# Attention and two MLPs in one kernel: places of their own, by tables, for attention's jobs and a step's operations

## The chip, the cores and the metric

The kernel runs on one core of a Trainium2 chip. The metric is the device time of one execution in microseconds. Three runs of the kernel before took 1445.11, 1445.52 and 1445.93 us; the median is 1445.52.

## The reference

Attention of 8 batches, 8 heads, 576 positions, head size 64, through 32 packed tokens per head, and then two MLPs on the 4608 tokens (width 512, hidden 2048), all in fp32:

```python
a = softmax(p @ k.T / 8) @ v          # 32 packed tokens per head
x = softmax(q @ a.T / 8) @ a          # 576 positions per head
h = x @ moe_w_in
g = where(h >= 1, h, where(h <= -1, 0, (h + 1)**2 / 4))
x = g @ moe_w_out
h = x @ moe2_w_in
out = (h * sigmoid(h)) @ moe2_w_out
```

## The kernel before

**Two stages.** The first stage (to about 750 us) computes attention and the first MLP, the second the second MLP (products of L842 and L904 on blocks of 512 and 384 tokens). The change touches the first stage alone. There the first MLP's input product is folded: the attention output is a weighted sum of 32 packed tokens per head, so the packed tokens are multiplied with `w_in` first (`wp8`, L566, and `wp_out`, L581, for each quarter f of the hidden width), and a step then multiplies the attention weights with the result.

**Steps.** One step is one half t of a batch (288 tokens) and one slice m of 128 hidden units: 8 x 2 x 16 = 256 steps, 32 per batch. Its operations are `a_h` (6 matmuls, L661, on TensorE), `a_relu` (two activations on ScalarE, L676 and L677), `a_max` (VectorE, L682), `a_hi` (ScalarE, L686) and `a_lo` (VectorE, L692), which split the result into a high and a low part, and `a_y` (12 matmuls, L707). Batch 0's first eight steps use one plain matmul per product instead (L703). In batch 0's first half of the slices the low parts are made by GpSimd.

**Attention's jobs.** While the steps of batch b-1 run, attention of batch b is computed by some 45 jobs, in two parts. The front: loads of p, k, v (SP's queue), scores of the packed tokens (`s1_8` and `s1_end8`, L264 and L276, matmuls of L270 and L281), copies and maxima, exponentials, transposes (`s1_tr`, `s1_trt`), the product with v (`pp_mm`, L364), its norm, transpose and copy into `pp`. The back: loads of q, the scores `s2_8` (L484) and `s2_end8` (L495), and for each of three tiles i: `t_in` (transpose, L509), `t_max` (L519, L520), `t_exp`, `t_norm` (L531 to L534), `t_out` (L539), `t_a2` (L553, L555); then `load_win`, `wp8` and `wp_out` for the four quarters. The names in the change are s1, s1e, cp, cpe, mx, ex, tr, trt, ce, cpt, rec, pp, nrm, ptr, pout, s2, s2e, ti, tm, te, tn, to, ta, w (wp8), wo (wp_out), and for loads lp, lk, lv, lq, lw.

**Order written out by a key.** Every piece of work is an event with a number, its key. The events are sorted by key and issued in that order, and each engine works through its own queue in that order; semaphores set by the framework hold an instruction back until its operands and its buffer are ready. Step i has `a_y` at i + 0.9, `a_h` at i - 3.7, `a_relu`, `a_max` at i - 2.69 and - 2.66, `a_hi` at i - 1.68, `a_lo` at i - 0.67 (`when`, L1200). Attention of batch b counts from base = 32 (b - 1): all jobs of a slot stand at one key with the fraction 0.6, and slots follow each other by one step: front from base + 2, back from base + 16, quarter f's `wp8` at base + 21.6 + 4f and `wp_out` one later, its two win loads three earlier (L1100 to L1127). Batch 1 has its own four numbers.

**The beginning.** Batch 0's attention, the conversion of the 64-bit weights (load `raw..`, first part on ScalarE `a..`, second part on VectorE `b..`, split `c..`, for w_in tiles `in0` to `in15` and w_out tiles `o0` to `o15`), and the first 20 steps have a key each in the table START. F and S are batch 0's front and back jobs, W its `wp` jobs. Short runs of filler matmuls (`fill`) stand between them.

**Second MLP's weights.** During the steps from 34 on, every 25 steps, the weights of the second MLP are loaded, converted and combined, in jobs on ScalarE and VectorE (`a_first` to `a_fourth`, L744 to L763, with the splits of L137), and stored by SP. Their keys are not changed.

**Buffers.** Pool `big` has 37 tiles of 4 KB per partition, for loads, weights and splits alike. Attention's and a step's matmuls share four PSUM banks (`bank`, L132); the banks of `a_y` are four others. `wp8` and `s2_8` take two banks each, `s2_end8` and `a_h` one.

Of the kernel before, what the change touches and what calls it, by code (L numbers as in the profile page):

```python
# [72 lines left out]
def attention_then_two_mlps(ctx: ExitStack, tc: tile.TileContext, kT, vv, qT, pT, w_in, w_out, w2_in, w2_out, out):  # L73
# [3 lines left out]
    B, P, NJ, S = kT.shape  # L77
# [7 lines left out]
    KF = DFF // P  # L85
# [162 lines left out]
    def att_jobs(b):  # L248
# [372 lines left out]
        def back(every=4, only=None):  # L621
# [7 lines left out]
            return jobs  # L629

        wps = [
            [[J(wp, f, g) for g in range(NG)] if b < 1 else [J(wp8, f)], [J(wp_out, f, g) for g in range(NG)]]
            for f in range(NF)
        ]
        return front, back, wps

    win_t = {}

    def store_win(f, g):
        win_t[1, f, g] = w_in_t[g, f]  # L640
        nc.sync.dma_start(win_dram[f, g], w_in_t[g, f])
# [316 lines left out]
    def slots(n, jobs, every=1):  # L958
        for i, slot in enumerate(jobs):
            for fn in slot:  # L960
                at(n + i * every, fn)
# [304 lines left out]
```

## Time and profile before

| what | value |
|---|---|
| median of three runs | 1445.52 us |
| the profiled execution | 1445.66 us, span 1443.6 us |
| instructions | 26352 |
| busy: TensorE, VectorE, ScalarE, GpSimd | 99%, 66%, 53%, 5% |
| granted TensorE clock | 1.00 in every slice |
| DMA | 300.32 MB, 208 GB/s over the span |

The span is the time from the first to the last instruction of one execution. Busy is the share of the span in which an engine's instructions run by the profile; matmul ends are modelled and overlap with the next start, so TensorE's share is no measure of what it could do. In a timeline each row is one or several merged instructions with their start and duration; the bracket behind it is the idle time of that engine just before, and what ended it. PEld is TensorE's weight load.

### The profile page before, as it was taken

The page shows a single profiled execution, that of the slowest core. Times are in us where ns is not written, and L with a number is a line of the kernel's source. Part 1 is how long each engine was busy: PE and PEld are TensorE (multiplying, and loading weights), DVE is VectorE, ACT ScalarE, POOL GpSimd, SP SyncE. Part 2 cuts the span into 40 slices and gives each one's busy share as a digit, 9 for nine tenths or more (in the row PEclk, how much of TensorE's full clock was granted, in tenths as well). Part 3 has the DMA queues.
Part 4 walks back from the last instruction along what each step waited for, and adds up shares of the span by engine and source line. Part 5 has one row for each costly group of instructions (what it writes and reads, how often), then busy time and mean ns, then how long its engine had stood idle before and what let it go on. Part 6 is the DMA issues. An engine that isn't in the chain of part 4 may idle for free.

```text
span 1443.6 us, 26352 instructions
## 1 busy us (share of the span) xinstructions
PE 1429.9 (99%) x9812; PEld 1280.5 (89%) x9812; DVE 951.3 (66%) x1711; ACT 766.2 (53%) x1536; POOL 74.8 (5%) x116
## 2 busy tenths in 40 slices
PE   8999999999999999999999999999999999999999
PEld 7778989989899898999998888888888889999998
DVE  5788586675867758577736775477646764774664
ACT  4776667676676767766653452334423541362342
POOL 0250000000000000000000000000000000000000
PEclk9999999999999999999999999999999999999999
DMA  9654545646464555545337677866787678888886
GB/s 346 230 199 131 195 163 185 230 156 222 153 223 162 187 179 190 192 156 185 105 93 241 193 208 222 267 191 193 230 258 195 193 222 281 260 269 285 253 252 223
DMA packets 178639, 300.32 MB, mean 208 GB/s; under 512 B 28624, under 2 KB 76752, under 8 KB 178512
## 3 DMA queue, kind: packets, MB, share of 16 engines
q1 hardware_dynamic: 167760, 264.36, 58.2%
q0 software_dynamic: 9344, 33.04, 6.7%
q8 instruction: 78, 1.28, 0.4%
q10 hardware_dynamic: 1408, 1.25, 0.3%
q14 instruction: 49, 0.40, 0.1%
HBM read 244.97 MB, written 53.61 MB: 207 GB/s over the span
## 4 chain that ended last, share of the span: by engine, by line
PE 90%; DVE 5%; DMA 2%; issue 1%; ACT 1%; POOL 0%; DVEq 0%; ACTq 0%; POOLq 0%
PE ps_y L707 25%; PE ps_o L904 24%; PE ps_h L842 22%; PE ps_h L661 12%; PE ps_wp L573 2%; PE ps_y L703 1%; PE ps_pp L364 1%; DMA qt<-qT 1%; DMA raw<-w_in 1%; DVE g L692 1%; DMA va<-vv 1%; PE ps_s L270 0%; DVE u L682 0%; DVE gt L887 0%; DVE w L154 0%
## 5 line engine op out<-in xcount | busy, mean ns | idle before, releaser
L707 PE MATMUL ps_y<-g,w_o 128*128 128x288 f32 x2976 | 443.8, 298 | 3.0 <-DVE g L692 1.8
L707 PEld LDWEIGHTS ps_y<-g,w_o 128*128 128x128 f32 x2976 | 407.7, 188 | 35.1 <-ACT u L676 10.1
L842 PE MATMUL ps_h<-y,a2r 128*128 128x512 f32 (+1 forms) x1680 | 347.7, 367 | 0.4 <-DVE p L868 0.2
L904 PE MATMUL ps_o<-g,a2r 128*128 128x512 f32 (+1 forms) x1680 | 345.8, 367 | 0.0
L842 PEld LDWEIGHTS ps_h<-y,a2r 128*128 128x128 f32 x1680 | 305.2, 188 | 40.9 <-DVE p L868 1.8
L904 PEld LDWEIGHTS ps_o<-g,a2r 128*128 128x128 f32 x1680 | 305.7, 188 | 39.2
L661 PE MATMUL ps_h<-a,wp 128*128 128x288 f32 x1536 | 246.2, 296 | 1.1 <-DVE u L682 0.4
L682 DVE SCALAR_TENSOR_TENSOR u<-ps_h,u 128x288 f32<-128x288 f32 x256 | 116.1, 455 | 160.2 <-ACT u L677 159.8
L661 PEld LDWEIGHTS ps_h<-a,wp 128*128 128x128 f32 x1536 | 217.3, 188 | 4.4 <-issue 1.6
L676 ACT ACTIVATE u<-ps_h,half 128x288 f32<-128x288 f32 x256 | 128.2, 501 | 171.4 <-PE ps_h L661 147.5
L677 ACT ACTIVATE u<-u 128x288 f32<-128x288 f32 x256 | 113.8, 445 | 8.1
L692 DVE TENSOR_TENSOR g<-u,g 128x288 fp32r<-128x288 f32 x240 | 109.6, 457 | 1.7 <-ACT g L686 1.7
L686 ACT CAST g<-u 128x288 fp32r<-128x288 f32 x248 | 103.5, 417 | 0.2 <-PE ps_y L703 0.2
L800 DVE TENSOR_TENSOR g<-gs,g 128x1024 fp32r<-128x1024 f32 (+1 forms) x80 | 86.7, 1112 | 7.4 <-ACT g L799 7.4
L863 ACT COPY p<-ps_h 128x512 f32<-128x512 f32 (+1 forms) x40 | 21.8, 545 | 124.1 <-PE ps_h L842 116.2
L799 ACT CAST g<-gs 128x1024 fp32r<-128x1024 f32 (+1 forms) x80 | 73.9, 962 | 8.6 <-PE ps_o L904 5.8
L868 DVE TENSOR_TENSOR p<-ps_h,p 128x512 f32<-128x512 f32 (+1 forms) x80 | 50.2, 633 | 39.9 <-PE ps_h L842 39.4
L800 DVE TENSOR_TENSOR g<-gt,g 128x1024 fp32r<-128x1024 f32 (+1 forms) x60 | 64.5, 1112 | 6.8 <-ACT g L799 6.8
L878 ACT ACTIVATE gs<-u 128x512 f32<-128x512 f32 (+1 forms) x40 | 23.6, 589 | 82.6 <-DVE u L868 82.6
L878 ACT ACTIVATE gs<-ps_h 128x512 f32<-128x512 f32 (+1 forms) x40 | 22.3, 556 | 63.3 <-PE ps_h L842 63.3
L799 ACT CAST g<-gt 128x1024 fp32r<-128x1024 f32 (+1 forms) x60 | 53.8, 963 | 0.5 <-PE ps_o L904 0.5
L645 POOL DMA_DIRECT2D win<-win_dram x48 | 25.5, 532 | 515.1 <-DVE g L692 113.2
(142 smaller groups left out, 1145.0 us busy)
## 6 DMA issues: line engine op xcount, KB each, us to landing
a2r<-a_dram SPq DMA_DIRECT2D x280, 256.0 KB, 3.0
a2r<-o_dram SPq DMA_DIRECT2D x280, 256.0 KB, 3.0
win<-win_dram POOLq DMA_DIRECT2D x48, 512.0 KB, 4.3
raw<-w_in SPq DMA_DIRECT2D x32, 512.0 KB, 7.4
raw<-w_out SPq DMA_DIRECT2D x32, 512.0 KB, 6.3
a_dram<-a2w SPq DMA_DIRECT2D x56, 256.0 KB, 2.8
o_dram<-a2w SPq DMA_DIRECT2D x56, 256.0 KB, 2.7
y_dram<-ysb SPq DMA_DIRECT2D x36, 288.0 KB, 2.5
```

The lines of the kernel that those rows point to most:

```text
L661: nc.tensor.matmul(ps[:, :HB], w[:, i, o:o + P], a2[:, k, g, :], start=(n == 0), stop=(n == 3 * NG - 1))
L676: nc.scalar.activation(u, h_ps[s][:, :HB], AF.Relu, bias=half, scale=0.5)
L677: nc.scalar.activation(u, u, AF.Square)
L682: nc.vector.scalar_tensor_tensor(u, h_ps.pop(s)[:, :HB], 1.0, u, op0=ALU.max, op1=ALU.min)
L686: nc.scalar.copy(g[:, 0], u_t[s])
L692: eng.tensor_tensor(g[:, 1], u_t.pop(s), g[:, 0].bitcast(F32), op=ALU.subtract)
L707: nc.tensor.matmul(acc["y"][d][:, :HB], w[:, i, d * P:(d + 1) * P], g[:, k], start=(first and n == 0), stop=(last and n == 2),)
L799: nc.scalar.copy(hi, src)
L800: nc.vector.tensor_tensor(lo, src, hi.bitcast(F32), op=ALU.subtract)
L842: nc.tensor.matmul(ps, w[:, x, a * P:(a + 1) * P], b_t[i, j][k][:, a], start=(n == 0 and j in FIRST), stop=(n == 3 * KH - 1), skip_group_c ...
L868: nc.vector.tensor_tensor(t, bk[*key, b][:, :w], x, op=ALU.add)
L904: nc.tensor.matmul(ps, w[:, x, d * P:(d + 1) * P], g[k][:, p % 2], start=(p == 0 and n == 0 and j in FIRST), stop=(p == NPR - 1 and n == 2 ...
```

## The change

Order alone; no instruction is added or taken away. Three tables give every attention job of batches 1 (first), 3, 5, 7 (odd) and 2, 4, 6 (even) a key of its own, counted from 32 (b - 1). Four tables give a step's operations theirs, by the parity of the step's batch and its half t (step00 to step11); they hold from step 20 on. START gets new numbers for 77 of its events. The table START is shown up to where batch 0's steps begin.

```diff
--- before.py
+++ after.py
 START = {
-    "p": -99.25, "k": -99.0, "v0": -98.0, "rawin1": -96.6, "rawin0": -96.5, "F0.0": -96.320312, "F1.0": -91.289062,
-    "F0.1": -91.269531, "F1.1": -91.25, "F2.1": -90.789062, "v1": -90.328125, "F1.2": -88.359375, "q0": -88.125,
-    "q1": -87.179688, "rawin3": -87.0, "F2.0": -86.625, "rawin2": -86.21875, "F3.0": -85.8125, "F3.1": -84.3125,
-    "rawo1": -81.5, "F4.0": -80.5, "rawo0": -80.0, "F4.1": -79.5, "F5.2": -74.4375, "F5.0": -74.277344,
-    "F6.1": -73.796875, "rawin7": -72.476562, "rawo2": -70.471094, "F5.1": -70.385547, "F6.0": -70.0875,
-    "rawin6": -69.854688, "F6.2": -69.662891, "ain0": -68.3, "F7.0": -62.234375, "rawin4": -62.1875,
-    "rawin5": -62.007812, "bin0": -61.828125, "ain1": -60.75, "F7.1": -60.28125, "rawo3": -59.0, "F8.0": -59.0,
-    "F9.0": -59.0, "F10.0": -57.25, "S0.0": -56.0, "ain2": -54.625, "bin1": -54.1875, "W0.0.0": -53.84375,
-    "S0.1": -53.5, "S0.2": -52.0, "bin2": -50.0, "ao0": -47.5625, "q3": -47.40625, "ain3": -47.25, "ao1": -46.5625,
...
+    "p": -99.25, "q0": -99.1875, "q1": -99.125, "k": -99, "rawin1": -96.6, "rawin0": -96.5, "F0.0": -96.320312,
+    "F1.0": -91.289062, "F0.1": -91.269531, "v0": -91.259766, "F1.1": -91.25, "F2.1": -90.789062, "v1": -90.328125,
+    "F1.2": -88.359375, "rawin3": -87, "F2.0": -86.625, "rawin2": -86.21875, "F3.0": -85.8125, "F3.1": -84.3125,
+    "F4.0": -80.5, "rawo0": -80, "rawo1": -79.75, "rawin7": -79.625, "F4.1": -79.5, "F5.2": -74.4375,
+    "F5.0": -74.277344, "F6.1": -73.796875, "rawo2": -70.471094, "F5.1": -70.385547, "F6.0": -70.0875, "ain0": -68.3,
+    "F7.0": -62.234375, "F6.2": -62.210938, "ain1": -62.199219, "rawin4": -62.1875, "rawin6": -62.097656,
+    "rawin5": -62.007812, "rawo3": -61.917969, "bin0": -61.828125, "F7.1": -60.28125, "F8.0": -59, "F9.0": -58.9,
+    "F10.0": -57.25, "S0.0": -56, "ain2": -54.625, "bin1": -54.1875, "ao1": -54.015625, "W0.0.0": -53.84375,
+    "S0.1": -53.5, "S0.2": -52, "bin2": -50, "ao0": -47.5625, "S0.3": -45.875, "S1.0": -45.5, "S1.1": -44.5,
+    "ain3": -44.34375, "S0.4": -44.1875, "S1.2": -44.15625, "bin3": -44.125, "W0.0.1": -40.96875,
...
+ORDER = {
+    "first": {
+        "lp": 0.9, "lk": 1.9, "lv0": 4.7, "s1": 4.9, "s1e": 4.91, "cp0": 5.9, "cpe": 5.91, "lv1": 6.9, "mx0": 6.91,
+        "cp1": 7.1, "ex0": 7.6, "mx1": 8.61, "tr0": 8.61, "ex1": 9.1, "tr1": 9.91, "ce0": 10.1, "trt": 10.12,
+        "ce1": 10.6, "cpt": 10.61, "rec": 10.62, "lq2": 10.7, "pp0": 11.6, "lq0": 11.7, "pp1": 11.91, "lq1": 12,
+        "nrm": 13.3, "ptr": 13.6, "pout": 16.6, "s2": 17.7, "s2e": 18.7, "ti1": 18.72, "ti0": 19.21, "tm0": 19.7,
+        "ti2": 20.21, "tm1": 20.71, "te0": 21.2, "tn0": 21.7, "w0": 21.8, "te1": 22.01, "to0": 22.2, "wo0": 23.3,
+        "w1": 24.1, "tn1": 24.71, "tm2": 24.72, "ta0": 24.8, "to1": 25.71, "te2": 25.72, "wo1": 26.3, "tn2": 26.51,
+        "ta1": 26.7, "w2": 27.1, "to2": 29, "wo2": 29.1, "ta2": 30.2, "w3": 32.3, "wo3": 33.3,
+    },
+    "odd": {
+        "lp": -1.3, "lk": 0.2, "lv1": 5, "s1": 5, "s1e": 5.01, "cpe": 5.71, "cp0": 6.5, "cp1": 7, "mx0": 7.01,
+        "mx1": 7.01, "lv0": 7.7, "ex0": 8, "lq0": 8.2, "tr0": 9.01, "ex1": 10, "ce0": 10, "tr1": 10.01, "trt": 10.02,
+        "lq1": 10.82, "ce1": 11, "cpt": 11.01, "pp0": 12, "pp1": 12.01, "rec": 12.4, "nrm": 13.2, "ptr": 13.5,
+        "pout": 14.2, "lq2": 15.5, "s2": 16.7, "ti0": 17.2, "s2e": 17.72, "lw0": 18, "tm0": 18.2, "ti1": 18.51,
+        "te0": 18.9, "tm1": 19.21, "ti2": 19.71, "w0": 20, "tn0": 20.2, "te1": 20.21, "tn1": 20.71, "to0": 20.72,
+        "tm2": 21.9, "wo0": 22.41, "lw1": 23.1, "to1": 23.6, "ta0": 24.5, "lw2": 24.6, "ta1": 25.51, "w1": 25.6,
+        "te2": 25.82, "tn2": 26.3, "to2": 27, "lw3": 27.8, "wo1": 27.9, "w2": 29.1, "ta2": 29.4, "wo2": 30.7,
+        "w3": 32.9, "wo3": 33.4,
+    },
+    "even": {
+        "lk": -1.9, "lp": -0.4, "lv0": 1.1, "lv1": 2.1, "s1": 2.1, "s1e": 2.11, "cpe": 3.1, "cp0": 4.11, "cp1": 5.1,
+        "mx0": 5.61, "ex0": 6.6, "mx1": 6.61, "ex1": 7.6, "tr0": 7.61, "lq2": 8.9, "ce0": 10.6, "tr1": 10.61,
+        "trt": 10.62, "lq1": 11.12, "rec": 11.6, "ce1": 12.31, "cpt": 12.4, "pp0": 12.6, "pp1": 12.9, "lq0": 13.61,
+        "nrm": 13.9, "ptr": 15.9, "pout": 16, "s2": 17.4, "s2e": 17.41, "ti1": 17.42, "lw0": 18.4, "ti0": 18.6,
+        "ti2": 19.3, "tm0": 19.31, "tm1": 19.91, "te0": 20.4, "w0": 21, "tn0": 21.9, "te1": 21.91, "wo0": 22,
+        "tn1": 22.9, "to0": 22.91, "tm2": 22.92, "to1": 23.82, "ta0": 23.9, "te2": 24.41, "tn2": 24.91, "ta1": 25.9,
+        "to2": 27.6, "lw1": 27.6, "lw2": 28.2, "w1": 28.4, "ta2": 28.9, "wo1": 29.6, "w2": 29.6, "lw3": 30.7,
+        "wo2": 31.2, "w3": 34.2, "wo3": 35.2,
+    },
+    "step00": {
+        "h": -3.7, "relu": -2.69, "max": -2.66, "hi": -1.68, "lo": -0.95, "y": 0.96,
+    },
+    "step01": {
+        "h": -3.72, "relu": -2.69, "max": -2.66, "hi": -1.68, "lo": -0.67, "y": 0.9,
+    },
+    "step10": {
+        "h": -3.72, "relu": -2.67, "max": -2.64, "hi": -2.36, "lo": -1.15, "y": 0.94,
+    },
+    "step11": {
+        "h": -3.76, "relu": -2.69, "max": -2.6, "hi": -1.68, "lo": -1.45, "y": 0.42,
+    },
 }
...
-        return front, back, wps
+        named = {
+            "s1": [s1_tiles, s1_8], "s1e": [s1_end8], "cpe": [s1_copy_end], "trt": [s1_trt], "cpt": [ett_copy],
+            "rec": [s1_rec], "nrm": [pp_norm], "ptr": [pp_tr], "pout": [pp_out], "s2": [s2_8], "s2e": [s2_end8],
+            **{
+                f"{k}{i}": [J(fn, i)] for k, fn, n in (
+                    ("cp", s1_copy, 2), ("mx", s1_max, 2), ("ex", s1_exp, 2), ("tr", s1_tr, 2), ("ce", et_copy, 2),
+                    ("pp", pp_mm, 2), ("ti", t_in, 3), ("tm", t_max, 3), ("te", t_exp, 3), ("tn", t_norm, 3),
+                    ("to", t_out, 3), ("ta", t_a2, 3), ("w", wp8, NF),
+                ) for i in range(n)
+            },
+            **{f"wo{f}": [J(wp_out, f, g) for g in range(NG)] for f in range(NF)},
+        }
+        return front, back, wps, named
...
-    G = dict(pf1=4, pb1=18, w1=0, pf=2, pb=16, pw=21, lw=3, lk=4, lv=-1, lq=6, ai=34, ad=25, oraw=1)
+    G = dict(w1=0, ai=34, ad=25, oraw=1)
...
-    def slots(n, jobs, every=1):
-        for i, slot in enumerate(jobs):
-            for fn in slot:
-                at(n + i * every, fn)
-
...
-        front, back, wps = att_jobs(0)
+        front, back, wps, _ = att_jobs(0)
...
-        def plan_front(b, n):
-            at(n - G['lk'], load_p, b)
-            at(n - G['lk'], load_k, b)
-            for g in range(NG):
-                at(n + G['lv'] + g, load_v, b, g)
-            slots(n, jobs[b][0])
-
-        def plan_back(b, n):
-            for g in range(NG + 1):
-                at(n - G['lq'] + min(g, 1), load_q8, b, g)
-            slots(n, jobs[b][1]())
-
-        jobs = {b: att_jobs(b) for b in range(1, B)}
-        plan_front(1, G['pf1'])
-        plan_back(1, G['pb1'])
+        def plan(b, q, order):
+            jobs = {
+                "lp": [lambda: load_p(b)], "lk": [lambda: load_k(b)],
+                **{f"lv{g}": [lambda g=g: load_v(b, g)] for g in range(NG)},
+                **{f"lq{g}": [lambda g=g: load_q8(b, g)] for g in range(NG + 1)},
+                **{f"lw{f}": [lambda f=f, g=g: load_win(b, f, g) for g in range(NG)] for f in range(NF) if b > 1},
+                **att_jobs(b)[3],
+            }
+            for name, fns in jobs.items():
+                for fn in fns:
+                    ev(q + order[name], fn)
+
         for f in range(NF):
             for g in range(NG):
                 at(KF + 4 * f + G['w1'] - 0.05, store_win, f, g)
-            slots(KF + 4 * f + G['w1'], jobs[1][2][f])
-        for b in range(2, B):
-            base = (b - 1) * SPB
-            plan_front(b, base + G['pf'])
-            plan_back(b, base + G['pb'])
-            for f in range(NF):
-                n = base + G['pw'] + 4 * f
-                for g in range(NG):
-                    at(n - G['lw'], load_win, b, f, g)
-                slots(n, jobs[b][2][f])
+        for b in range(1, B):
+            plan(b, (b - 1) * SPB, ORDER["first" if b == 1 else "odd" if b % 2 else "even"])
...
-        def when(n, rank, fn, step):
-            ev(n + (0.9 if rank == 9 else 0.3 + 0.01 * rank), fn, step)
...
-                    when(h, 0, a_h, step)
-                    when(h + 1, 1, a_relu, step)
-                    when(hi, 2 if hi > h + 1 else 5, a_hi, step)
-                    when(lo, 3 if lo > hi else 6, a_lo, step)
-                    when(h + 1, 4, a_max, step)
-                    when(i, 9, a_y, step)
+                    order = ORDER[f"step{step[0] % 2}{step[1]}"]
+                    for name, fn in (("h", a_h), ("relu", a_relu), ("hi", a_hi), ("lo", a_lo), ("max", a_max), ("y", a_y)):
+                        ev(i + order[name], fn, step)
```

## Rows read from the trace of the kernel before

**Rows 1.** The page: the chain that ended last, shares of the span by engine
```profile
PE 90%; DVE 5%; DMA 2%; issue 1%; ACT 1%; POOL 0%; DVEq 0%; ACTq 0%; POOLq 0%
```

**Rows 2.** Timeline of TensorE (start, duration, instructions): first scores of batches 2 to 7
```profile
148.77 1.09 PE L270 MATMUL ps_s<-kt,pbd 64*32 64x512 f32 x16
...
238.10 1.09 PE L270 MATMUL ps_s<-kt,pbd 64*32 64x512 f32 x16
...
326.07 1.09 PE L270 MATMUL ps_s<-kt,pbd 64*32 64x512 f32 x16
...
415.56 1.09 PE L270 MATMUL ps_s<-kt,pbd 64*32 64x512 f32 x16
...
503.53 1.09 PE L270 MATMUL ps_s<-kt,pbd 64*32 64x512 f32 x16
...
592.56 1.09 PE L270 MATMUL ps_s<-kt,pbd 64*32 64x512 f32 x16
```

**Rows 3.** Timeline of TensorE's weight loads: those that waited for VectorE
```profile
212.94 0.18 PEld L573 LDWEIGHTS ps_wp<-win,pp 64*32 64x32 f32 x14 [1.10 <-DVE u L682]
...
387.08 0.30 PEld L707 LDWEIGHTS ps_y<-g,w_o 128*128 128x128 f32 x2 [0.49 <-DVE g L692]
...
390.39 0.18 PEld L573 LDWEIGHTS ps_wp<-win,pp 64*32 64x32 f32 x14 [0.70 <-DVE u L682]
...
561.25 0.30 PEld L661 LDWEIGHTS ps_h<-a,wp 128*128 128x128 f32 x2 [0.69 <-DVE u L682]
```

**Rows 4.** Groups by line on VectorE (count | busy us, mean ns | idle before)
```profile
L682 DVE SCALAR_TENSOR_TENSOR u<-ps_h,u 128x288 f32<-128x288 f32 x256 | 116.1, 455 | 160.2 <-ACT u L677 159.8
L692 DVE TENSOR_TENSOR g<-u,g 128x288 fp32r<-128x288 f32 x240 | 109.6, 457 | 1.7 <-ACT g L686 1.7
...
L532 DVE TENSOR_SCALAR r<-r 128x4 f32<-128x4 f32 x7 | 1.2, 170 | 0.2
```

**Rows 5.** Timeline of TensorE: two steps of batch 4, one with batch 5's s2e
```profile
456.56 0.96 PE L661 MATMUL ps_h<-a,wp 128*128 128x288 f32 x6
457.44 0.43 PE L495 MATMUL ps_s2e<-qte,pp 128*32 128x64 f32 x16
457.81 1.85 PE L707 MATMUL ps_y<-g,w_o 128*128 128x288 f32 x12
459.50 0.96 PE L661 MATMUL ps_h<-a,wp 128*128 128x288 f32 x6
460.29 1.77 PE L707 MATMUL ps_y<-g,w_o 128*128 128x288 f32 x12
461.90 0.96 PE L661 MATMUL ps_h<-a,wp 128*128 128x288 f32 x6
```

**Rows 6.** Timeline of VectorE and of TensorE's weight loads around batch 1's back
```profile
99.84 1.29 DVE L137 TENSOR_TENSOR wp<-ps_wp,wp 128x512 fp32r<-128x512 f32 x2 [0.54 <-ACT wp L136]
...
102.60 0.43 PEld L707 LDWEIGHTS ps_y<-g,w_o 128*128 128x128 f32 x3 [1.80 <-DVE g L692]
...
109.69 0.27 PEld L495 LDWEIGHTS ps_s2e<-qte,pp 128*32 128x32 f32 x16 [1.20 <-DVE u L682]
```

**Rows 7.** Timeline of ScalarE and VectorE at the start
```profile
21.34 0.63 ACT L433 ACTIVATE e<-e 128x512 f32<-128x512 f32 x1 [1.90 <-DVE e L428]
22.20 1.25 ACT L147 ACTIVATE raw<-raw 128x512 f32<-128x512 f32 x2 [0.23 <-DMA raw<-w_out]
...
21.75 0.69 DVE L154 SCALAR_TENSOR_TENSOR w_in<-raw 128x512 uint32<-128x512 uint32 x1
...
39.33 0.69 DVE L154 SCALAR_TENSOR_TENSOR w_in<-raw 128x512 uint32<-128x512 uint32 x1 [0.51 <-ACT raw L147]
```

**Rows 8.** Batch 2's last win load and its use; DMA issues with us to landing
```profile
206.81 0.53 POOL L645 DMA_DIRECT2D win<-win_dram  x1 [3.96 <-PE ps_h L661]
...
234.50 1.09 PE L573 MATMUL ps_wp<-win,pp 64*32 64x512 f32 x16
...
win<-win_dram POOLq DMA_DIRECT2D x48, 512.0 KB, 4.3
```

More of the change, by code (lines that the diff above doesn't have):

```diff
@@ L1098, in attention_then_two_mlps @@
         job("part1", 2 * KF - 5 + .67, load_part, 0, 1)
-        def plan_front(b, n):
-            at(n - G['lk'], load_p, b)
-            at(n - G['lk'], load_k, b)
-            for g in range(NG):
-                at(n + G['lv'] + g, load_v, b, g)
-            slots(n, jobs[b][0])
-        def plan_back(b, n):
-            for g in range(NG + 1):
-                at(n - G['lq'] + min(g, 1), load_q8, b, g)
-            slots(n, jobs[b][1]())
-        jobs = {b: att_jobs(b) for b in range(1, B)}
-        plan_front(1, G['pf1'])
-        plan_back(1, G['pb1'])
+        def plan(b, q, order):
[5 more added lines that the diff above has]
+                **att_jobs(b)[3],
+            }
+            for name, fns in jobs.items():
+                for fn in fns:
+                    ev(q + order[name], fn)
         for f in range(NF):
```

73 rows, old and new, of the table START are left out of this document.

## The prediction

> **What bounds the kernel now.** I read the page first: busy time and the chain of waits. TensorE is busy nearly throughout and the chain lies on it for 90% of the span [rows 1], so a job moved on ScalarE, VectorE or a queue is worth time only where TensorE waits for it. Matmul ends are modelled and overlap, so a wait hides inside "busy"; I therefore went on by start times. Attention of batch b is spread over the 32 steps of batch b-1, and each batch runs the same instructions. The starts of its first scores (L270) for batches 2 to 7 [rows 2] lie 89.33, 87.97, 89.49, 87.97 and 89.03 us apart. The stretches of batches 3 and 5 agree to 0.01 us; those of 2, 4 and 6 are longer by 1.36, 1.52 and 1.06, 3.94 us together. The timeline of TensorE's weight loads says where: waits of 1.10, 0.49, 0.70 and 0.69 us, each for VectorE's max (L682) or its low part (L692), all some 60 us behind these starts [rows 3]. From about 690 us, where attention's last jobs end, only hi, lo and y of the last steps have new places.
>
> So VectorE runs late there. I added up what it is given between one step's max and the next, with each group's mean ([rows 4] are the first two and the last, by busy time, of the 31 groups used), and set it against TensorE's time for the step: 2.39 us (0.79 for L661 and 1.60 for L707 [rows 5]) plus attention's matmuls. For batch 2, steps 53 to 58: 3.83 + 2.28 + 3.93 + 3.95 + 5.29 + 3.91 = 23.2 us given in 16.1 us, so VectorE is 7.1 us late at step 58. The tail of attention (three normalisations, wo0) meets there four jobs that prepare the second MLP's weights. The same sum gives 6.9 us for batch 4 and 6.3 for batch 6, but at most 2.6, 3.6 and 4.8 for batches 3, 5 and 7, whose preparation falls elsewhere and where TensorE waits for nothing. Lateness less lost time is 5.7, 5.4 and 5.2: about what buffers and banks absorb.
>
> **The change, part by part.**
>
> A. *Places of attention's jobs of batches 2, 4, 6, and of hi and lo.* Counted out by the new tables, batch 2's steps 53 to 58 give VectorE 22.1 us (ta1 and tn2, 1.75 us, go to later steps, one ti of 0.69 comes in) in 17.3 us (s2 and s2e, 1.2 us more of TensorE, now fall inside). Lateness: 4.8, at most 5.0 two steps later; batch 4: 5.6; batch 6: 4.6. Two of three are under the 5.2 to 5.7 that was absorbed, batch 4 touches it. w1, which takes two banks at once and stood at 212.94 and 390.39 [rows 3], moves from 25.6 to 28.4, where the sum has VectorE no longer late. In odd batches lo comes about one step earlier, so a step's L707 has 2.4 us more before its operand can be late. I take 3.94 less 0.2 for batch 4: -3.7 us. Bounds: -3.94 (all of it) and -2.0 (half stays, because the preparation jobs stay where they are).
>
> B. *s2 and s2e side by side for batches 2, 4, 6* (17.4 and 17.41; before, a step apart). Around a block of plain fp32 matmuls TensorE loses time twice: L661 before it takes 0.88 instead of 0.79, L707 behind it 1.69 instead of 1.61 [rows 5]. One pair less: 0.17 x 3 = -0.5 us. It cannot be more; a bank that is not yet free would give it back (bound 0).
>
> C. *Batch 1's own table.* Before, wo0 (1.29 us on VectorE at 99.84) lay ahead of the lo for which TensorE waited until 102.60 (1.80 us); and s2e waited 1.20 us for a max at 109.69 [rows 6]. wo0 now comes six steps later: -1.3. s2e now takes a bank that the max before that one frees: -1.2. What is late next: step 24's hidden product needs the bank that ti0 frees, and ti0 now stands behind bo14 (about 1.2 us: L153 and L154) and a lo. Adding these in order from 102.5 us, ti0 ends some 1.8 us after TensorE is there: +1.8. Sum -0.7; bounds -2.5 (ti0 in time) and +1.5.
>
> D. *The start.* Raw weights land one behind the other; the first two of w_out were o1, o0 and are now o0, o1. ScalarE's conversion ao1 now stands ahead of S0.2, batch 0's first exponential. That one started at 21.34; the second raw tile of w_out landed for 22.20 [rows 7]. So ao1 takes 22.20 to 22.87 (0.67 each, two in 1.25), and S0.2 starts 1.5 us later; VectorE, done at 22.44 with the conversion behind S0.1 (21.75 + 0.69), stands still until about 23.5. It is then busy into the thirties, so the 1.1 us is carried to the conversion that TensorE's W1.0.0 needs; there VectorE itself waited 0.51 us at 39.33 [rows 7], which takes up half. +0.6 us; bounds -0.1 and +1.5. Queries ahead of keys on SP, and batch 0's first values later: the bytes ahead of batch 0's second keys stay the same (q0 and q1 take the place of one value tile), so 0, and inside those bounds. y0 ahead of the filler matmuls: 0, because W1.0.0 behind them waits for VectorE anyway.
>
> ScalarE's place in D is where a rule speaks against the change. "PSUM — Partial Sum Buffer", section "Engine vs sequencer instructions", of the Trainium skill says that ScalarE's queue is strictly first in, first out. By it S0.2 waits for ao1 the whole 1.5 us whatever its own operand does, and a price of 1.5 in place of 0.6 would make the sum 0.9 us worse. The trace does not contradict it: the rows show ScalarE idle 1.90 us ahead of S0.2 [rows 7].
>
> E. *The other moves of START* (weight conversions, W2, co4, y8 to y11) lie at 40 to 100 us. I cost them at 0: each goes past one or two neighbours on its own queue, and TensorE has its own work in front of it there. If that cover is gone, or a wait goes that I don't see, it is about one wait of the size of [rows 3]: -1.0 to +1.0.
>
> F. *Loads and queues.* p, keys, values and queries pass SP's stores of prepared weights by a step or two, and win's loads on GpSimd's queue move by up to five steps. No instruction is added. GpSimd issues a load when its buffer is free, well ahead of its place: batch 2's last one at 206.81, used at 234.50 [rows 8], with its place three steps (7.2 us) before the use, so 20 us ahead. Landing takes 4.3 us [rows 8]. 0; if that lead were gone, see the second rival.
>
> Sum: -3.7 - 0.5 - 0.7 + 0.6 = -4.3 us. The profiled execution took 1445.66 us (span 1443.6), 0.14 above the median of the runs: 1445.52 - 4.3 = 1441.2 us.
>
> **The rivals.**
>
> *The waits come back elsewhere.* Three sums rest on how late VectorE may be before TensorE notices, and in batch 1 and at the start the new order puts work ahead of something that is waited for. With A at -2.0, B -0.5, C +0.5 and D +1.1: 1444.6 us, no change that can be told. For it: the same VectorE work, the same collision with the preparation jobs, and a lateness in batch 4 at the limit. Against: the lateness falls in all three batches, and w1 leaves the worst place.
>
> *A win load comes late (slower).* In even batches w1's loads now stand at 27.6 and w1 at 28.4, 0.8 steps or 1.9 us. If GpSimd were to issue them only at their place, two issues of 0.53 us and 4.3 us to land [rows 8] make 5.3 us, 3.4 us too late, in each of three batches: 10.2 us, and 1441.2 + 10.2 = 1451.4. It decides from a lead under 5.3 us. Against it: the 20 us of lead above; buffers are fewer only if more tiles live at once, and fewer win tiles do.
>
> *The start costs its full price.* By the rule of D, with S0.2's delay carried whole to step 0, D is +1.5 and E, whose moves stand behind it, +1.0: 1441.2 + 0.9 + 1.0 = 1443.1.
>
> *The change does nothing:* the tables would have to give the old order, and read out side by side they don't (w1 stands three steps later in even batches).
>
> **How the numbers follow.** Forecast 0.66, waits that come back 0.20, full price at the start 0.08, late loads 0.06. 0.2% is 2.9 us, about what a measurement of this kernel can tell from no change, so faster means under 1442.6 and slower over 1448.4. The forecast's own range is 1438.0 to 1443.5, with one part in twenty of it above 1442.6: faster 0.63 + some of the start's rival (0.03) = 0.66; slower 0.06; the rest, 0.28, the same. All bounds at their best (A -3.94, B -0.5, C -2.5, D -0.1, E -1.0) give 1437.5. The range for 8 in 10 is 1437.5 to 1445.0: it takes in the first rival's time and leaves out the late loads and the best and worst corners.
>
> **What would show it.** Right: L270's starts of batches 2 to 7 (with their new places) fit stretches of 87.4 to 88.2 us everywhere; no weight load of TensorE waits over 0.3 us for L682 or L692 between 200 and 600 us; L484 and L495 adjacent for batches 2, 4 and 6; in batch 1 one wait near 108 us for a transpose (L509) in place of those at 102.60 and 109.69; at the start ScalarE idle until 22.2, the exponential after it, and W1.0.0 some 0.6 us later. Wrong: waits for VectorE near 390 us as before (A), L573 waiting for a DMA (F), or the first L270 of batch 2 at more than 150 us after allowing for its place half a step earlier (C, D, E).

## The result, and the profile after

The changed kernel takes 1455.01 us (median of 6 runs, 1450.41 to 1455.88) against 1445.51 for the kernel before beside it: ratio 1.0061, interval 1.0048 to 1.0074. Forecast were 1441.2 us and a range of 1437.5 to 1445.0, so sign and range were wrong. The profiled run took 1454.68 us. Lines of code stand 45 to 57 higher than before: L270 is now L315, L661 is L718, L682 and L692 are L739 and L749, L707 is L764.

The page: span, busy times, TensorE's granted clock in 40 slices, the chain by engine.
```profile
span 1452.9 us, 26341 instructions
PE 1430.8 (98%) x9812; PEld 1284.4 (88%) x9812; DVE 952.4 (66%) x1711; ACT 770.3 (53%) x1536; POOL 75.6 (5%) x116
...
PEclk8999999999999999999999999999999999999999
...
PE 93%; DVE 3%; DMA 1%; ACT 1%; issue 1%; SPq 0%; POOL 0%; DVEq 0%; ACTq 0%; POOLq 0%
```
The chain lies on TensorE even more than before [rows 1]; the page only hints at the loss, by the 8 in PEclk's first slice. First scores of batches 2 to 7, to be read beside [rows 2]:
```profile
161.34 1.09 PE L315 MATMUL ps_s<-kt,pbd 64*32 64x512 f32 x16
...
256.30 1.09 PE L315 MATMUL ps_s<-kt,pbd 64*32 64x512 f32 x16
...
336.96 1.09 PE L315 MATMUL ps_s<-kt,pbd 64*32 64x512 f32 x16
...
431.97 1.09 PE L315 MATMUL ps_s<-kt,pbd 64*32 64x512 f32 x16
...
512.64 1.09 PE L315 MATMUL ps_s<-kt,pbd 64*32 64x512 f32 x16
...
607.60 1.09 PE L315 MATMUL ps_s<-kt,pbd 64*32 64x512 f32 x16
```
Odd batches now begin some three steps later in their stretch than even ones, so stretches are read in pairs: batch 2 to 4 and 4 to 6 take 175.62 and 175.68 us instead of 177.30 and 177.46. The steady part gained; but batch 2 starts 12.57 us late although its place is half a step earlier, which is the sign that the forecast had named against its parts C, D and E (later than 150 us). The chain of waits over the first 48 us shows where that begins (start, duration, what):
```profile
8.24 1.03 PE ps_s L304 x4
9.30 11.77 DMA va<-vv
21.07 0.14 issue
21.21 1.45 PE ps_pp L409 x40
22.66 1.15 PE ps_fill L1027 x4
```
va is v0, half of batch 0's values, the one load of values that goes through ScalarE's queue. It stands behind ScalarE's first copy of scores, which needs the first keys, so it is issued at 9.30 and lands at 21.07; before, it was issued at 1.92 and had landed at 8.04. Two more views show the consequences: the waits of SP's queue from 8 to 25 us, and the table of stretches (busy time of PE, PEld, DVE, ACT, POOL, then granted clock, DMA share, GB/s).
```profile
SPq L215 <- DMA va<-vv: 7.5, 1, 7.5
```
```profile
15.00:20.00 5.00, 0.09 (x1) 0.00 (x0) 0.72 (x2) 2.20 (x5) 0.00 (x0) 0.98 1.03 365
20.00:25.00 5.00, 3.79 (x84) 3.04 (x84) 0.00 (x0) 0.89 (x2) 0.00 (x0) 0.50 0.63 189
25.00:30.00 5.00, 4.45 (x48) 3.82 (x42) 2.19 (x6) 0.00 (x0) 0.00 (x0) 0.50 1.00 381
30.00:35.00 5.00, 5.00 (x43) 3.93 (x40) 4.72 (x11) 1.77 (x3) 0.00 (x0) 1.00 1.07 380
```
SP stands still for 7.5 us until v0 has landed, although its next load is a raw weight tile. The trace says why: in the order of the keys, loads wait here for the landing of the load eight places before them, whatever its queue. The two tiles ahead start at 11.91 and 13.26, 0.02 us after two such landings (11.89 and 13.24), and this one, the eighth behind v0, at 21.09. TensorE has nothing to do from 15 us on, and once v0 is there its granted clock is 0.50, the lower of its two levels. The first hidden product (first ps_h from here on) starts at 40.31 us, not 28.91: 11.40 us late. Further on, TensorE's timeline has two waits that the forecast had smaller or not at all (matmuls; the wait before them in brackets):
```profile
121.30 1.11 PE L718 MATMUL ps_h<-a,wp 128*128 128x288 f32 x6 [3.12 <-DVE e L554]
...
644.17 0.43 PE L540 MATMUL ps_s2e<-qte,pp 128*32 128x64 f32 x16 [1.07 <-DMA qte<-qT]
```

### The profile page after: what moved, and what is told of

Read it like the earlier page. It is cut to its first block, busy times and chain, and to the rows that moved or that the text cites. A ratio compares the mean times of both kernels' runs of the same rounds, so it can differ in the third digit from the quotient of the medians.

```text
span 1452.9 us, 26341 instructions
## 1 busy us (share of the span) xinstructions
PE 1430.8 (98%) x9812; PEld 1284.4 (88%) x9812; DVE 952.4 (66%) x1711; ACT 770.3 (53%) x1536; POOL 75.6 (5%) x116
## 4 chain that ended last, share of the span: by engine, by line
PE 93%; DVE 3%; DMA 1%; ACT 1%; issue 1%; SPq 0%; POOL 0%; DVEq 0%; ACTq 0%; POOLq 0%
PE ps_y L764 26%; PE ps_o L961 24%; PE ps_h L899 22%; PE ps_h L718 14%; PE ps_wp L618 2%; PE ps_y L760 1%; PE ps_pp L409 1%; DMA va<-vv 1%; DVE raw L198 1%; DMA qte<-qT 1%; PE ps_s L315 0%; DVE gt L944 0%; PE ps_et L374 0%; DVE w L199 0%; PE ps_s L529 0%
## 5 line engine op out<-in xcount | busy, mean ns | idle before, releaser
L764 PE MATMUL ps_y<-g,w_o 128*128 128x288 f32 x2976 | 440.8, 297 | 1.4 <-POOL g L749 1.4
L764 PEld LDWEIGHTS ps_y<-g,w_o 128*128 128x128 f32 x2976 | 409.2, 189 | 16.1 <-ACT u L733 5.0
L718 PE MATMUL ps_h<-a,wp 128*128 128x288 f32 x1536 | 250.3, 299 | 3.4 <-DVE e L554 3.1
L718 PEld LDWEIGHTS ps_h<-a,wp 128*128 128x128 f32 x1536 | 218.3, 189 | 21.0 <-DVE g L749 4.2
L739 DVE SCALAR_TENSOR_TENSOR u<-ps_h,u 128x288 f32<-128x288 f32 x256 | 116.0, 454 | 151.1 <-ACT u L734 149.4
L749 DVE TENSOR_TENSOR g<-u,g 128x288 fp32r<-128x288 f32 x240 | 109.4, 456 | 3.7 <-ACT g L743 3.7
```

What stands on the lines that cost most here:

```text
L718: nc.tensor.matmul(ps[:, :HB], w[:, i, o:o + P], a2[:, k, g, :], start=(n == 0), stop=(n == 3 * NG - 1))
L739: nc.vector.scalar_tensor_tensor(u, h_ps.pop(s)[:, :HB], 1.0, u, op0=ALU.max, op1=ALU.min)
L749: eng.tensor_tensor(g[:, 1], u_t.pop(s), g[:, 0].bitcast(F32), op=ALU.subtract)
L764: nc.tensor.matmul(acc["y"][d][:, :HB], w[:, i, d * P:(d + 1) * P], g[:, k], start=(first and n == 0), stop=(last and n == 2),)
```

## The experiments

All times are medians; the kernel before took 1445.34 to 1445.67 beside them. Several of these kernels scatter by 3 to 5.5 us: the lower clock follows the wait near 110 us, below, in some profiles and not in others, and batch 7's wait for a load comes and goes. So between neighbours I read the traces' first ps_h and not the medians alone. Each kernel has one trace; the four with the old START in full (before, e4, e7, e11) have their first ps_h between 28.65 and 29.02, so a difference under 0.4 us says nothing.

**The change in halves.** One kernel has the new START alone, one the new tables alone; two more move only v0.
```
e1: after,  START "v0": -91.259766 -> -98.0
e2: before, START "v0": -98.0 -> -91.259766
e3: before, with the new START
e4: after,  with the old START
```


> The changed kernel with one entry of START put back: v0 (batch 0's first values) at -98.0 again, so that ScalarE issues this load before its first copy. Theory V (the late v0 is what lost the time): v0 is issued near 2 us instead of 9.30 and lands by 10 instead of 21.07, TensorE's first ps_pp matmul starts near 14 to 15, its first ps_h at 29 to 31 instead of 40.31, and the time falls by about 11 us, from 1455.0 to 1444 (1442.5 to 1446). Rival Q (the queries that now stand ahead of keys on SP's queue fill the engines, whoever issues v0): v0 lands no earlier than 16 and the time stays over 1451. Rival T (batch 1's and the later tables lost it): the start gets shorter but under 3 us of the time come back.

> The kernel before with one entry of START changed: v0 at -91.259766, behind ScalarE's first copy of scores; all other places as before. Theory V: v0 is issued at 9.5 to 10.5 us, stands beside a full SP queue, lands at 18 to 22, the first ps_h comes 8 to 12 us later than 28.91, and the time is 1453 to 1457. Rival Q (late v0 hurts only together with the queries ahead of keys): v0 lands by 16, the first ps_h is under 4 us later, the time under 1449.5.

> The kernel before with the whole new START table, attention's jobs of batches 1 to 7 and the steps' operations at the old places. Theory V: the loss of the start without the gain of the later tables: first ps_h at 39 to 41 us, no wait of 3 us near 121, waits of VectorE in batches 2, 4 and 6 as before, 1445.5 + 11.4 = 1457 (1455.5 to 1458.5). Rival T: the start alone costs under 3 us, 1446 to 1448.5.

> The changed kernel with the whole old START table, the new tables for batches 1 to 7 and for the steps' operations kept. Theory V: first ps_h near 28.9 us; places in batches 2, 4 and 6 bring the -3.6 to -4.2 us that they were forecast to bring, batch 1's own table loses 1 to 2.5 us in the wait for its first transpose (3.1 us in the changed kernel's trace) and gains less than that elsewhere: 1442.5 to 1444.5. The forecast of batch 1's table (-0.7) right: 1441.2. Rival T: 1450 or more.

Measured: e1 1445.09 (ratio 1.0001, 0.9993 to 1.0010), e2 1452.59 (1.0044, 1.0030 to 1.0058), e3 1456.93 (1.0072, 1.0060 to 1.0085), e4 1441.17 (0.9967, 0.9955 to 0.9980). The whole loss is START's. The tables alone come within 0.6 us of what A, B and C were forecast to bring (1440.6); that they hit the 1441.2 forecast for everything is chance. e4's own expectation took off more for batch 1 and missed. The halves do not add up (11.6 less 4.2 is 7.4, not 9.5): matched ps_h by ps_h with e4's, the changed kernel's profile loses another 1.8 us between the products that the kernel before has at 105 and at 122 us, at the wait at 121.30 and the lower clock behind it, and 1.1 us at batch 7's s2e. v0's place alone costs the kernel before 7.2 us (issued 9.55, landed 18.96, first ps_h 36.56), a little less than the range expected, and from 45 us on its profile stays 7.45 us behind. Put back, it gives the changed kernel 9.9 us, but its first ps_h comes only to 32.94, missing the 29 to 31 expected: something else in START costs 4 us.

**What else is in START.**
```
e5:  e1 with "q0", "q1": -99.19, -99.13 -> -88.125, -87.179688
e6:  e5 with "ao1": -54.015625 -> -46.5625
e10: e6 with "bo1": -40.262695 -> -6.675
```


> The changed kernel with v0, q0 and q1 back at their old places in START (-98.0, -88.125, -87.179688); the rest of the new START kept. With v0 alone back the time was 1445.1, 3.9 us over the old START with the new tables (1441.2), and the second keys (kt on SP) landed at 11.10 instead of about 9.6. Theory V+Q (the queries ahead of the keys hold the second keys and, through the loads that wait for an earlier landing, the second half of v0 back): kt lands by 9.7, first ps_pp before 15, first ps_h at 29.5 to 30.5 instead of 32.94, time 1441.5 to 1443.0. Rival S (ScalarE's ao1 ahead of the first exponential, or the moves of 40 to 100 us, cost the 3.9): the first ps_h stays at 32 us or later, or it comes early and the time is still 1444 or more.

> As the kernel with v0, q0 and q1 back, and ao1 back at -46.5625, behind batch 0's first exponential: the difference between the two is the price of ao1's place (step D's only term). Forecast of D: 0.6 us (-0.1 to 1.5), so this kernel is 0.6 us faster, and the exponential starts near 21.3 instead of 22.9. Rival (full price): 1.5 us faster. Rival (w_out's raw tile arrives late anyway and nothing waits): within 0.2 us of each other.

> The kernel with v0, q0, q1 and ao1 back, and bo1 (VectorE's two operations for w_out's second tile, 1.03 us) back from -40.26 to -6.675, behind the normalisation that the first hidden product waits for. Theory B (bo1's new place is what is left of the start's loss; the old START and this kernel differ in their first ps_h by 2.1 us): first ps_h at 28.7 to 29.7 instead of 30.78, granted clock 1.00 from 25 to 40 us instead of 0.66 in 30 to 35, time 1441.5 to 1443. Rival (several small moves, none of them over 0.5 us): first ps_h stays over 30.2 us, time 1443.8 to 1445.

First ps_h: 30.58, 30.78, 29.41 us; times 1445.65, 1444.36 and 1443.38. By these, beside an early v0, the queries ahead of the keys cost 2.4 us (second keys landed at 9.90 instead of 11.10), ao1 nothing (0.2 the other way), bo1 1.4. e5's time did not follow its start, so that half of its expectation missed and the time is where its rival S had it: its profile falls back by 4.5 us against the kernel before between 105 and 122 us (ps_h matched one by one), e1's by 1.9, both behind the same wait for a transpose, with a granted clock of 0.52 from 110 to 115 us in e5 and of 1.00 in e1. So the times do not settle ao1's price: e5's and e6's medians lie 1.3 us apart, the way of a price, in runs that scatter by 5. Their traces do not settle it either, for in e5 the raw tile that ao1 waits for landed early, at 21.33 us (22.18 in e6). The kernel e12, described below, has ao1 at its new place and this tile at 22.83 us; ScalarE's and VectorE's timelines there:
```profile
22.85 0.69 ACT L192 ACTIVATE raw<-raw 128x512 f32<-128x512 f32 x1 [3.13 <-DMA raw<-w_out]
23.43 0.62 ACT L478 ACTIVATE e<-e 128x512 f32<-128x512 f32 x1
...
24.09 0.69 DVE L486 TENSOR_REDUCE r<-e 128x16 f32<-128x512 f32 x1 [0.86 <-ACT e L478]
```
The exponential stands behind ao1, and VectorE waits 0.86 us for it, on the chain that ends in the first ps_h: what D had priced. bo1 is to be seen in VectorE's timeline, e6 first, then e10:
```profile
27.12 0.68 DVE L519 TENSOR_TENSOR a<-ps_tr,a 128x512 fp32r<-128x512 f32 x1
27.72 0.42 DVE L198 TENSOR_SCALAR raw<-raw 128x512 uint32<-128x512 uint32 x1
28.17 0.69 DVE L199 SCALAR_TENSOR_TENSOR w<-raw 128x512 uint32<-128x512 uint32 x1
28.79 0.40 DVE L486 TENSOR_REDUCE r<-e 32x8 f32<-32x256 f32 x1
```
```profile
26.83 0.68 DVE L519 TENSOR_TENSOR a<-ps_tr,a 128x512 fp32r<-128x512 f32 x1
27.43 0.40 DVE L486 TENSOR_REDUCE r<-e 32x8 f32<-32x256 f32 x1
```
L198 and L199 (w) are bo1, 1.07 us from start to next start. They stand ahead of the normalisation (L486 on) that the last transposes, and so the first ps_h, wait for. From first ps_pp to first ps_h e10 takes 1.07 us less than e6; the other 0.3 of the 1.4 lies ahead of that. e10's time is 0.4 us over its range.

**The queue, and the clock.** e12 leaves v0 at its late place and sends it through SP's queue; e8 and e9 keep TensorE busy while it waits.
```
e12: load_v:  eng = nc.sync if b or g else nc.scalar  ->  eng = nc.sync
e8:  fill list: + (-62.3, 105)
e9:  fill list: + (-62.3, 28)
```


> The changed kernel with one word changed: batch 0's v0 goes through SP's queue, as all other loads of values, instead of ScalarE's, at its new place in the order. Theory G (SP's later loads wait for the landing of a load eight before them, and a transfer on ScalarE's queue gets a small share beside SP's: 11.8 us in flight against 8.4 for v1): v0 is issued near 9.2 to 11 and lands at 16.5 to 18.5 instead of 21.07, SP's pause of 7.5 us goes, first ps_h at 35 to 38, time 1449.5 to 1453. Rival (the place alone counts, the queue does not): v0 lands at 20 or later, time 1454 to 1456.

> The changed kernel with 105 filler matmuls (128x128 of the identity, into a bank that nobody reads) put into TensorE's queue ahead of the first ps_pp matmuls, so that TensorE works while it waits for v0. They add no wait for data. Theory W (the granted clock, 0.50 from 20 to 30 us after the wait, costs about 3 us up to the first ps_h: the blocks from ps_pp to the second scores take 2.9 us longer than in the kernel with v0 back): the granted clock stays 1.00 up to 30 us, v0 lands at 21.1 as before, first ps_h at 37 to 38 instead of 40.31, time 1451.5 to 1452.8. Rival (loads and VectorE set the first ps_h, the clock hides in their waits): clock restored, first ps_h within 0.7 us of 40.31, time 1454 to 1455.5.

> The same trial with 28 filler matmuls: 105 of them took 23.61 us (0.225 each) and ended 16 us after v0 had landed, so that trial measured the filler. 28 take 6.3 us and end near 21.5, with v0 at 21.1. Theory W (the granted clock of 0.50 after the wait costs about 3 us up to the first ps_h): granted clock 1.00 up to 30 us, first ps_h at 37.5 to 38.5 instead of 40.31, time 1452 to 1453. Rival (loads and VectorE set the first ps_h anyway): clock restored, first ps_h within 0.7 us of 40.31, time 1454 to 1455.5.

e12 took 1446.63 us (1.0002, 0.9993 to 1.0010), below its range: one word gives back 8.4 of the 9.5 us lost. v0 is issued at 8.41, lands at 16.40, SP waits for values 1.5 us at most, first ps_h 32.06. With v0 issued late, but on SP's queue, TensorE waits for it only twice, 0.33 and 0.41 us. So the late issue by itself is the smaller part; the transfer on ScalarE's queue beside a full SP queue is the larger. The DMA view of the changed kernel from 9 to 22 us (queue: packets, MB, share of 16 engines) shows the division:
```profile
q1 hardware_dynamic: 1444, 3.59, 75.9%
q10 hardware_dynamic: 608, 0.59, 14.5%
```
q10 is ScalarE's queue, q1 SP's: v0 and its tail were 0.59 of 4.18 MB, a seventh; SP's tiles moved the rest. The Trainium skill, "DMA: Bandwidth & Descriptors", section "Queues, rings and completion order", says that each DMA engine takes turns between its queues packet by packet. If the profile's packets are those, the trace doesn't agree: 608 to 1444 while both had work for most of the time.

e8 was mis-sized: 105 fillers took 23.61 us and ended over 16 us after v0 had landed; its 1468.11 us (1.0155) measure the filler. e9's 28 took 6.4, and it ran 1450.43 us (1.0032, 1.0020 to 1.0045), 4.6 below the changed kernel and under its range. Its stretches, to set beside those above:
```profile
15.00:20.00 5.00, 5.00 (x47) 5.00 (x46) 0.82 (x2) 2.56 (x5) 0.00 (x0) 1.00 1.02 380
20.00:25.00 5.00, 4.19 (x99) 3.35 (x99) 0.61 (x2) 0.68 (x1) 0.00 (x0) 1.00 0.52 149
25.00:30.00 5.00, 4.93 (x61) 3.83 (x62) 4.01 (x8) 1.24 (x3) 0.00 (x0) 1.00 1.00 358
```
v0 landed at 21.57, half a microsecond later than in the changed kernel, yet first ps_h came at 37.74, in the range expected. From the first ps_pp that is 16.04 us (21.70 to 37.74) instead of 19.10 (21.21 to 40.31): the lower clock cost 3.06 us there. The lead at first ps_h, 2.57 us, is unchanged at 600 us (2.55); the rest of the gain comes at batch 7, whose wait of 1.07 us for a load is absent from e9's profile, and is not due to the clock at the start.

**Two places in the tables.**
```
e7:  e4 with first "ti0": 19.21 -> 18.73
e11: e7 with odd "lq2": 15.5 -> 10.83
```


> The old START with the new tables (1441.2 us) and one more place changed: in batch 1's table ti0 stands at 18.73 instead of 19.21, so VectorE does this transpose ahead of bo14 and of a low part. Theory C (TensorE's wait of 3.0 us at 109.63 is for these two jobs ahead of ti0): the wait falls under 0.7 us, the next wait in line takes back up to 1 us, time 1438 to 1440. Rival (another of VectorE's late jobs or bo14's user takes the wait over): 1440.7 to 1441.7.

> The old START with the new tables, ti0 at 18.73 in batch 1's table, and lq2 at 10.83 instead of 15.5 in the table of odd batches, so that SP issues the tail of the queries ahead of stores that wait for VectorE. Theory L (in batch 7 this 64 KB load, issued at 622.00 and landed at 630.74, made the s2e block wait 1.7 us, and a lower clock followed): no wait of s2e for a load in any odd batch, time 1438 to 1439.8 and runs closer together than 1439.1 to 1443.0. Rival (the wait moves to VectorE, or the load delays something else on SP): 1440 to 1441.5.

e7 took 1440.74 us (0.9967, 0.9954 to 0.9979), e11 1439.27 (0.9953, 0.9940 to 0.9967; 5 runs within 0.7). In e7 the wait for ti0 is gone and 1.4 us for a low part (L749) stands in its place, more than the 1 us at most that was expected, and the time is where the rival had it, 0.4 us from e4's and not to be told from it. Its profile, of its slowest run, is 0.7 us ahead of e4's up to 600 us and then loses 3.3 us in batch 7, whose s2e waits for the queries' tail, followed by the lower clock (0.50 from 632 to 634 us; e4's profile has no such wait):
```profile
614.73 7.22 SPq L796 DMA_DIRECT2D o_dram<-a2w  x5
622.00 0.65 SPq L268 DMA_DIRECT2D qte<-qT  x1
```
```profile
630.87 0.43 PE L540 MATMUL ps_s2e<-qte,pp 128*32 128x64 f32 x16 [1.70 <-DMA qte<-qT]
```
SP issues that load behind five stores which wait for VectorE, and it lands 8.7 us later. Put ahead of them, no s2e waits for a load. e11 beats both kernels, by 6.4 us and 15.7 us.

## Why the prediction was wrong

*A and B were right as a sum.* No matmul between 200 and 600 us waits for an engine any more (before: three, of 0.2 to 0.4 us). The sign as I had worded it, no weight load waiting over 0.3 us for L682 or L692, is not met: nine gaps of 0.84 us bear these two names (now L739 and L749). The kernel before has gaps of this length too, most of them named after ScalarE, and no matmul waits behind them. Two pairs of stretches gave 3.5 us in the changed kernel; 2.88 of waits less 0.2, and 0.34 for s2 and s2e side by side, were forecast for these (3.0). With the old START, TensorE is level with the kernel before at batch 1's end (-0.06 us at 184) and 4.7 us ahead at 700: 4.6 against the 4.2 of A and B. B by itself was not tried. w1's win loads were never late: that rival had no part in it.

*C had the right place and the wrong size.* wo0's wait and s2e's went, and ti0 came late, by 3.12 us instead of 1.8 (2.84 with the old START). The added-up 1.2 us for bo14 and 0.45 for the low part took 2.1 and 1.5:
```profile
116.36 0.70 DVE L554 STREAM_TRANSPOSE e<-ps_s 128x512 f32<-128x512 f32 x1
116.99 1.39 DVE L198 TENSOR_SCALAR raw<-raw 128x512 uint32<-128x512 uint32 x1
118.49 0.69 DVE L199 SCALAR_TENSOR_TENSOR w<-raw 128x512 uint32<-128x512 uint32 x1
119.10 1.52 DVE L749 TENSOR_TENSOR g<-u,g 128x288 fp32r<-128x288 f32 x1
120.54 0.70 DVE L554 STREAM_TRANSPOSE e<-ps_s 128x512 f32<-128x512 f32 x1
```
```profile
116.81 1.29 POOL L241 TENSOR_TENSOR w_o<-w,w_o 128x512 fp32r<-128x512 f32 x1 [2.21 <-ACT w_o L239]
118.86 2.89 POOL L241 TENSOR_TENSOR w_o<-w,w_o 128x512 fp32r<-128x512 f32 x2 [0.76 <-ACT w_o L239]
```
VectorE's two long operations run beside GpSimd's subtractions; a mean over 240 low parts, 457 ns [rows 4], hides that. In the changed kernel the granted clock then fell to 0.54 (122 to 124 us), so this wait cost more than itself. Together with the gains C came out near 0 at a full clock, inside its bounds.

*D failed, and with it the forecast.* The step is the sentence "Queries ahead of keys on SP, and batch 0's first values later: the bytes ahead of batch 0's second keys stay the same ... so 0". I asked only what the later v0 does to the second keys and not when v0 itself lands. Its issue now waits for ScalarE's copy (9.30 us); it flies beside SP's tiles; and the idle TensorE comes back at half its clock. It holds SP's queue as well, but the chain of waits has no load between v0's landing and the first ps_h, so that pause is not on it. By first ps_h v0's late place cost 7.4 us (40.31 to 32.94), some 3 of them clock. The bytes ahead of the second keys were the same, q0 and q1 (576 KB) for v0 with its tail; but SP issues the queries first, the keys at 4.19 us instead of 2.86, and they landed at 10.61 instead of 9.70. That, too, is one trace: e8 and e9, with the same loads ahead, had them at 9.43 and 10.71. The term that I did price, ao1, at 0.6, had nothing to hold up in the changed kernel: its raw tile landed at 22.08 us, and the exponential waited for its operand until 31.3. With v0 in time it depends on that landing: 0 in e5, whose exponential began at 21.96 and not at 22.9, and 0.86 us of VectorE in e12, near the 1.1 that I had reckoned there.

*E was one move short.* "Each goes past one or two neighbours" is not true of bo1, which went from behind step 0's first work to ahead of its last normalisation, nor does it lie at 40 to 100 us: it runs at 27.72 us, and cost 1.4. *F* held for the win loads and failed for lq2 of batch 7, 1.07 us: in odd batches this load moved from 11.6 to 15.5, four steps and not "a step or two".

Sum by first ps_h, from the new START to the old with the new tables: 7.4 + 2.4 - 0.2 + 1.4 + 0.7 (moves not tried one by one) = 11.7 us, 40.31 to 28.65. The parts hold for this order of moves alone: in e12 the queries stand ahead of the keys as well, and with v0 late the second keys still landed at 9.78 and the first ps_pp came at 14.59 (14.43 in e5). How v0's lateness divides between issue and flight stays open: e12 issues it 0.9 us earlier and shortens the flight from 11.8 to 8.0 us at once. So does what decides whether the clock falls behind the same 3.1 us wait.

## What to carry to other kernels

When a load moves, follow the load itself: which instruction on its queue it now stands behind, what is in flight when it is issued, when it lands, and which later loads wait for that. "The same bytes" is an answer about its neighbours only. A wait that empties TensorE is to be priced with the clock that follows, and a sum of mean durations on VectorE with what GpSimd does at that time.

## What the runs showed of the hardware

A 512 KB load took 11.8 us on ScalarE's queue beside SP's tiles, and 8.0 on SP's own queue, issued 0.9 us earlier among nearly the same tiles. After a wait of 6.12 us for v0 TensorE was granted 0.50, as after those of 4.67 us in e2 and 5.29 in e3. After one of 3.12 us it was granted 1.00 in one kernel (e1), and after one of 3.13 us 0.52 in another (e5); of the eight profiles with this wait at 3.11 to 3.13 us, seven show the fall.

VectorE's L749 took 1.52 us beside GpSimd's subtraction instead of 0.46, L198 1.39 instead of 0.42, but a transpose out of a bank (L554) 0.70 as ever. The Trainium skill, "SBUF — State Buffer", section "SBUF: two separate sides", says that these two engines share one pair of ports, held for a whole instruction by whichever comes first, where VectorE's operation reads two operands from SBUF, and GpSimd's reads there too, or runs in a mode with two ports; the other waits. The trace agrees for L749, which reads two, and for L554, which reads a bank and was not held; L198 reads one, and whether a mode with two ports is what held it no run here shows.
